# A list-scheduled beginning and one burst of k-v products per batch, in a linear-attention and SwiGLU kernel

## Chip, cores, metric

The kernel runs on one NeuronCore of a Trainium2 chip. The metric is the device time of one execution in microseconds (us), as the median of several. A trace's span is 1.8 us shorter than the device time of the same execution; positions below are us from the start of the span. Experiments ran on different chips, so each kernel is compared with the runs of the kernel before from its own rounds.

## The reference

Eight batches, eight heads, 576 positions, head size 64, float32 inputs. Cosine-weighted linear attention, then a SwiGLU block over 4608 tokens with d_model 512 and d_ff 1536:

```python
def phi(x, c, s):                       # c, s: cos and sin of pi/2 * position / S
    r = np.maximum(x, 0.0)
    return np.concatenate([r * c, r * s], axis=-1)
q_p = phi(q, cos_w, sin_w);  k_p = phi(k, cos_w, sin_w)
kv  = np.einsum('bhsf,bhsd->bhfd', k_p, v)
num = np.einsum('bhsf,bhfd->bhsd', q_p, kv)
den = np.einsum('bhsf,bhf->bhs', q_p, np.sum(k_p, axis=2))[..., None] + 1e-06
x   = (num / den)                       # then tokens x 512
g = x @ w_gate
out = (g / (1 + np.exp(-g)) * (x @ w_val)) @ w_out
```

## The kernel before

I read the program text as the schedule: in the traces an engine takes its instructions in the order in which the program issues them (in the changed kernel's first trace VectorE stands 2.37 us before a cast whose input is late, with a copy behind it in the text whose own input, matmul sums, is done by 11.0 us). PSUM stands in the program as eight banks of 512 float32 to a partition, and every matmul line of the traces writes to them (`banks<-`). 128 tokens make a tile, four tiles a token group; the first group (tiles 0 to 3, batch 0) is the beginning that the change rewrites. Banks of PSUM are handed out by hand:

```python
banks = psum.tile([P, 8, 512], FP32, name="banks")
def take(n, hold=None): ...       # the n banks used longest ago, in program order
```

The first loads, on SyncE's queue: v, then k and q in turns (q of slots 0 and 1 belongs to tile 0, slots 2 and 3 to tile 1; a slot is 64 positions). GpSimd's queue loads the weights with conversion to bf16, and q of slots 4 to 8 (tiles 2 and 3, and the last slot of the batch) between them. An FFN column is 128 of the 1536 columns of d_ff:

```python
load_first("v", slice(0, 2)); load_first("v", slice(2, 4))
load_first("k", slice(0, 2))
load_first("q", slice(0, G), 0, 2)
load_first("k", slice(2, 4))
load_first("q", slice(0, G), 2, 4)
# ... (cut)
load_w(0, 1); load_w(1, 1)                 # columns 0 and 1 of w_gate and w_val
load_slots(0, "q", CUT[0], NC)
for i in (2, 4, 6): load_w(i)
```

The beginning handles a tile at a time, with products of zeros (`idle_products`) where TensorE (PE) would wait:

```python
# ... (cut: ReLU of the first k, casts of the first q)
kv_first(0); turn_q(0); idle_products(4)
relu_first_k(2, "dve"); relu_first_k(3, "act", 5, NC); relu_first_k(3, "dve", 0, 5)
weight_q(0); kv_first(1); cast_q(2, "act")
a_tile(0, split=True); cast_q(3, "act"); idle_products(4)
x_turn(0, fast="split"); turn_q(1); weight_q(1)
for f in range(2): ffn_mm(0, f, 0, 2)      # FFN columns 0 and 1 of tile 0
a_tile(1)
# ... (cut: tiles 2 and 3 in the same way, each followed by FFN columns)
```

In the later batches the k-v products (36 matmuls of 64 x 64 for each half j of the heads) stand in two slots, one FFN column apart:

```python
def kv_mm(b, j):
    if j == 0: st[b, "kvps"] = take(2, ("kv", b))
    for c in range(NC):
        for i in range(2):
            for e in range(2):
                # ... (cut)
                nc.tensor.matmul(out=..., lhsT=raws[b, "k"][es, g, c], rhs=v2s[b % 2][es, g, c, :, 0:D1], ...)
# ... (cut)
tk = (s0 + 4, s0 + 5)
for j in range(J): at(tk[j], lambda b=b, j=j: kv_mm(b, j))
```

Of the kernel before, what the change touches and what calls it, by code (L numbers as in the profile page):

```python
# [17 lines left out]
def kernel(  # L18
# [86 lines left out]
    CUT = (4, 5)  # L105
# [11 lines left out]

    load_first("v", slice(0, 2))
    load_first("v", slice(2, 4))
    load_first("k", slice(0, 2))  # L120
    load_first("q", slice(0, G), 0, 2)
    load_first("k", slice(2, 4))
# [143 lines left out]
    def kv_mm(b, j):  # L266
        if j == 0:
            st[b, "kvps"] = take(2, ("kv", b))
        ps = st[b, "kvps"]
        for c in range(NC):  # L270
            for i in range(2):
                for e in range(2):
                    es = slice(e * SH, (e + 1) * SH)
                    g = 2 * j + i
                    nc.tensor.matmul(  # L275
                        out=ps[i * D:(i + 1) * D, e, j * 2 * D1:(j + 1) * 2 * D1],
                        lhsT=raws[b, "k"][es, g, c],
                        rhs=v2s[b % 2][es, g, c, :, 0:D1],
                        start=(c == 0), stop=(c == NC - 1),
                    )  # L280
# [22 lines left out]
    def kv_first(j):  # L303

        ps = take(2)
        for e in range(2):
            nc.tensor.matmul(out=ps[:, e, 0:4 * D1], lhsT=zeros,
                             rhs=zeros[:, 0:D1].unsqueeze(1).to_broadcast([P, 4, D1]), start=True, stop=False)
        pv = ps[:, :, 0:4 * D1].rearrange("p e (w i x) -> p e w i x", w=2, i=2)
        for c in range(NC):  # L310
# [9 lines left out]
        for e, eng in enumerate((nc.scalar.copy, nc.vector.tensor_copy)):  # L320
            eng(out=kvd[0][:, e, j].rearrange("p w i x -> p (w i x)"), in_=ps[:, e, 0:4 * D1])
# [10 lines left out]
    def turn_q(t):  # L332
        ps = take(1).bitcast(BF16).rearrange("p (y e s) -> p y e s", e=2, s=SH)
        for j in range(J):
            for c in range(2):
# [5 lines left out]
                for i in range(2):  # L341
                    nc.tensor.transpose(out=ps[i * D:(i + 1) * D, y].rearrange("p e s -> p (e s)"),
                                        in_=raws[0, "q"][:, 2 * j + i, 2 * t + c], identity=ident)
        nc.scalar.activation(out=qr[t % 2].rearrange("p e j c s -> p e (j c) s"),
                             in_=ps[:, 0:2 * J].rearrange("p y e s -> p e y s"), func=AF.Relu)

    def weight_q(t):
        for w in range(2):
            nc.vector.tensor_tensor(
                out=qwT[t % 2][:, w].rearrange("p e j c s -> p (e j) (c s)"),  # L350
                in0=qr[t % 2].rearrange("p e j c s -> p (e j) (c s)"),
                in1=tabq[:, w, 2 * t:2 * t + 2].rearrange("p c s -> p (c s)").unsqueeze(1).to_broadcast([P, 2 * J, P]),
                op=ALU.mult)

    def a_tile(t, split=False):
        ps = take(2)
        for j in range(J):
            for e in range(2):
                for w in range(2):
                    nc.tensor.matmul(  # L360
                        out=ps[:, e, 2 * j * D1:2 * (j + 1) * D1],
                        lhsT=qwT[t % 2][:, w, e, j].rearrange("p c s -> p (c s)"),
                        rhs=kvd[0][:, e, j, w].rearrange("p i x -> p (i x)"),
                        start=(w == 0), stop=(w == 1),
                    )
        x_of(t, ps, split)
# [19 lines left out]
    def x_of(t, ps, split=False):  # L386
        num = ps[:, :, 0:2 * J * D1].rearrange("p e (y x) -> p e y x", x=D1)
        den = smp.tile([P, H, 1], FP32, name="den")
        dv = den.rearrange("p (e y) o -> p e y o", e=2)
        nc.vector.tensor_single_scalar(out=dv, in_=num[:, :, :, D:D1], scalar=1e-6, op=ALU.add)  # L390
        rec = smp.tile([P, H, 1], FP32, name="rec")
        nc.vector.reciprocal(out=rec, in_=den)
        rv = rec.rearrange("p (e y) o -> p e y o", e=2)
        x = xp.tile([P, d_model], BF16, name="x")
        xv = x.rearrange("p (y e d) -> p e y d", e=2, d=D)
        for ys in (slice(0, 2), slice(2, 4)) if split else (slice(0, 4),):
            nc.vector.tensor_tensor(  # L397
                out=xv[:, :, ys], in0=num[:, :, ys, 0:D],
                in1=rv[:, :, ys].to_broadcast([P, 2, ys.stop - ys.start, D]), op=ALU.mult)
        st["x", t] = x  # L400
# [45 lines left out]
    def x_turn(t, fast=False):  # L446
        x = st.pop(("x", t))
        tg, off = divmod(t, GH // 2)
        if tg not in xT:
            xT[tg] = xtp.tile([P, GH // 2, KC, P], BF16, name="xT")  # L450
        o = xT[tg][:, off]
        if fast == "split":
            for ks, eng in ((slice(0, 2), nc.scalar.copy), (slice(2, 4), nc.vector.tensor_copy)):
                ps = take(1).bitcast(BF16).rearrange("p (k x) -> p k x", x=P)
                for kc in range(ks.start, ks.stop):
                    nc.tensor.transpose(out=ps[:, kc], in_=x[:, kc * P:(kc + 1) * P], identity=ident)
                eng(out=o[:, ks], in_=ps[:, ks])
        elif fast:
            ps = take(1).bitcast(BF16).rearrange("p (k x) -> p k x", x=P)
            for kc in range(KC):  # L460
                nc.tensor.transpose(out=ps[:, kc], in_=x[:, kc * P:(kc + 1) * P], identity=ident)  # L461
            nc.scalar.copy(out=o, in_=ps[:, 0:KC])
        else:
            nc.sync.dma_start_transpose(out=o, in_=x)


    def ffn_mm(tg, fc, lo=0, hi=GH):
# [3 lines left out]
        fs = slice(fc * P, (fc + 1) * P)  # L471
        if 2 * n <= 512:
            both = take(1)
            ps = [both[:, 0:n], both[:, n:2 * n]]
        else:
            ps = [take(1)[:, 0:n] for _ in range(2)]
        for o, w in zip(ps, (wg_sb, wv_sb)):
            for kc in range(KC):
                nc.tensor.matmul(out=o, lhsT=w[:, kc, fs], rhs=xT[tg][:, ts, kc],  # L479
                                 start=(kc == 0), stop=(kc == KC - 1))  # L480
        st["f", tg, fc, lo] = ps

    def ffn_act(tg, fc, lo=0, hi=GH):
        n = (hi - lo) * SH
        ps = st.pop(("f", tg, fc, lo))
        sg = sgp.tile([P, T], BF16, name="sg")
        nc.scalar.activation(out=sg[:, 0:n], in_=ps[0], func=AF.Silu)  # L487
        r = lo * SH
        nc.vector.tensor_tensor(out=hts[tg % 2][:, fc, r:r + n], in0=sg[:, 0:n], in1=ps[1], op=ALU.mult)  # L489

    def ffn_fc(*a):
        ffn_mm(*a)
# [42 lines left out]
    for g in range(1, G):  # L535
        nc.scalar.copy(out=raw_of(0, "v")[:, g], in_=first["v"][:, g])  # L536
    for g in range(G):
        vmul(0, g)
    hold = consts.tile([P, 1], FP32)
    hold2 = consts.tile([1, 2], BF16)  # L540
    nc.gpsimd.tensor_copy(out=hold, in_=first["v"][:, 1, 0, 0:1])
    load_w(0, 1)
    load_w(1, 1)
    load_slots(0, "q", CUT[0], NC)
# [3 lines left out]
    load_w(8)  # L548
    load_w(10)
# [3 lines left out]
    load_wo(1)  # L553
    load_slots(1, "q", CUT[1], NC)
    load_wo(2)
# [25 lines left out]
    relu_first_k(0, "act")  # L581
    relu_first_k(1, "dve")
    cast_q(0, "dve")
    cast_q(1, "dve")
    kv_first(0)
    turn_q(0)
    idle_products(4)
    relu_first_k(2, "dve")
    relu_first_k(3, "act", 5, NC)
    relu_first_k(3, "dve", 0, 5)  # L590
    weight_q(0)
    kv_first(1)
    cast_q(2, "act")
    a_tile(0, split=True)
    cast_q(3, "act")
    idle_products(4)
    x_turn(0, fast="split")
    turn_q(1)
    weight_q(1)
    for f in range(2):  # L600
        ffn_mm(0, f, 0, 2)
    a_tile(1)
    for f in range(2):
        ffn_act(0, f, 0, 2)
    turn_q(2)
    weight_q(2)
    ffn_fc(0, 2, 0, 2)
    x_turn(1, fast=True)
    ffn_fc(0, 3, 0, 2)
    a_tile(2)  # L610
    turn_q(3)
    ffn_fc(0, 0, 2, 4)
    ffn_fc(0, 1, 2, 4)
    weight_q(3)
    ffn_fc(0, 2, 2, 4)
    x_turn(2, fast=True)
    ffn_fc(0, 3, 2, 4)
    a_tile(3)
# [3 lines left out]
    for f in range(0, FC, 2):  # L622
        order += [("a", g) for g in ((4, 5, 6), (7, 8), (9, 10), (11,), (), ())[f // 2]]
        order += [("b", g) for g in (f, f + 1)]
    at("a5", turn(3, True))
    for j in range(J):
        at("b1", lambda j=j: qturn_pe(0, j, NC - 1, NC, "act"))
# [4 lines left out]
    at("b9", lambda: kv_mm(1, 0))  # L632
    at("b10", lambda: kv_mm(1, 1), lambda: kv_out(1))
    at("b11", q_(1, 0, 0), q_(1, 1, 0))
# [4 lines left out]
    at((1, 0), turn(4, True), q_(1, 0, 1), a_(6, 0))  # L639
    at((1, 1), a_(6, 1), q_(1, 1, 1))  # L640
    at((1, 2), turn(5, True), a_(7, 0))
    at((1, 3), a_(7, 1))
    at((2, 0), turn(6, True))
    at((2, 2), turn(7, True))
# [17 lines left out]
    for b in range(2, B):  # L662
# [15 lines left out]
        for j in range(J):  # L678
            at(tk[j], lambda b=b, j=j: kv_mm(b, j))
        at(tk[-1], lambda b=b: kv_out2(b))  # L680
# [54 lines left out]
```

## Time and profile before

| | before |
|---|---|
| median | 331.71 us |
| span of the profiled execution | 329.4 us |
| PE busy | 322.2 us (98%) |
| first FFN product / second token group starts | 15.03 / 58.92 us |
| from there to the end | 270.49 us |

Up to "the second token group starts" (the first FFN product with 512 columns) lies everything that the new list orders. From there to the end the program is the same in both kernels but for the k-v bursts. So a trace splits into two numbers that can be read apart. On PE's timeline of the kernel before (start, length, engine, line, operation): the first FFN product and the first of the second group; the prediction shows the other lines on which its reading rests.

```profile
15.03 0.52 PE L479 MATMUL banks<-xT,wg_sb 128*128 128x128 bf16 x4
58.92 1.03 PE L479 MATMUL banks<-xT,wg_sb 128*128 128x512 bf16 x4
```

### The profile page before, as it was taken

The numbers are of one execution on the slowest core, as the hardware profiler recorded it, in microseconds if no ns is written. First come the engines' busy times: TensorE is split into PE (matmuls) and PEld (weight loads), VectorE is DVE, ScalarE is ACT, GpSimd is POOL, SyncE is SP. The second block draws the span as 40 slices with busy tenths as digits, with TensorE's granted clock in tenths as the row PEclk, the third lists the DMA queues.
The fourth block names the chain that finished last, engine by engine and source line by source line (L and its number), as shares of the span: only waits on it lengthen the run. The fifth ranks groups of instructions, "written<-read, shape, count | busy, mean of one in ns | idle before, by whom it ended". The sixth has DMA issues, their size and how long they took to land.

```text
span 329.4 us, 6225 instructions
## 1 busy us (share of the span) xinstructions
PE 322.2 (98%) x2484; PEld 165.1 (50%) x2484; DVE 182.5 (55%) x366; ACT 134.3 (41%) x252; POOL 33.3 (10%) x56
## 2 busy tenths in 40 slices
PE   8889999999999999999999999999999999999995
PEld 4578855454445444544444444544454444444443
DVE  7775758685655755475556655664664145413420
ACT  7545457753364334433433434343432033213311
POOL 6654200002000200020002000200000000000000
PEclk9999999999999999999999999999999999999999
DMA  7999998298858797969597959795932411341014
GB/s 276 217 200 200 205 207 165 64 131 125 174 110 112 111 161 156 126 92 190 135 134 114 173 118 136 106 192 103 140 47 49 98 32 30 36 99 31 0 32 96
DMA packets 70860, 40.51 MB, mean 123 GB/s; under 512 B 45616, under 2 KB 65328, under 8 KB 70832
## 3 DMA queue, kind: packets, MB, share of 16 engines
q1 hardware_dynamic: 49536, 22.55, 39.2%
q0 software_dynamic: 21136, 17.44, 34.9%
q8 instruction: 19, 0.31, 0.4%
q10 hardware_dynamic: 160, 0.13, 0.1%
q14 instruction: 9, 0.07, 0.1%
HBM read 37.75 MB, written 9.44 MB: 143 GB/s over the span
## 4 chain that ended last, share of the span: by engine, by line
PE 89%; DMA 8%; POOL 1%; ACT 0%; ACTq 0%; issue 0%
PE banks L479 54%; PE banks L506 28%; DMA wv_sb<-in_moe_w_val_dram 4%; DMA wg_sb<-in_moe_w_gate_dram 3%; PE banks L275 3%; PE banks L379 2%; DMA wo_sb<-in_v_dram 1%; PE banks L414 1%; PE banks L525 0%; POOL wg_sb L200 0%; PE banks L461 0%; POOL wv_sb L201 0%; PE banks L261 0%; ACT ob L528 0%; POOL raw_q L101 0%
## 5 line engine op out<-in xcount | busy, mean ns | idle before, releaser
L489 DVE TENSOR_TENSOR ht<-sg,banks 128x512 bf16<-128x512 bf16 (+2 forms) x124 | 76.3, 617 | 73.8 <-PE banks L479 63.6
L487 ACT ACTIVATE sg<-banks 128x512 bf16<-128x512 f32 (+2 forms) x124 | 67.2, 542 | 117.5 <-PE banks L479 112.6
L479 PE MATMUL banks<-xT,wv_sb 128*128 128x512 bf16 (+2 forms) x496 | 113.7, 352 | 1.0 <-DMA wv_sb<-in_moe_w_val_dram 1.0
L479 PE MATMUL banks<-xT,wg_sb 128*128 128x512 bf16 (+2 forms) x496 | 113.9, 352 | 0.3 <-DMA wg_sb<-in_moe_w_gate_dram 0.3
L506 PE MATMUL banks<-wo_sb,ht 128*128 128x512 bf16 x420 | 94.3, 379 | 0.0
L479 PEld LDWEIGHTS <-wv_sb 128*128 128x128 bf16 x496 | 47.4, 98 | 47.7 <-DMA wv_sb<-in_moe_w_val_dram 1.5
L479 PEld LDWEIGHTS <-wg_sb 128*128 128x128 bf16 x496 | 45.5, 98 | 41.5 <-DMA wg_sb<-in_moe_w_gate_dram 0.4
L506 PEld LDWEIGHTS <-ht 128*128 128x128 bf16 x420 | 40.0, 98 | 45.4 <-issue 0.4
L513 ACT COPY ob<-banks 128x512 f32<-128x512 f32 x18 | 10.5, 585 | 51.6 <-PE banks L506 49.6
L229 DVE TENSOR_TENSOR r_q<-raw_q,tab 128x1152 bf16<-128x1152 bf16 x24 | 17.9, 753 | 20.2 <-ACT raw_q L212 20.2
L513 DVE COPY ob<-banks 128x512 f32<-128x512 f32 x17 | 11.7, 691 | 28.6 <-PE banks L506 27.6
L233 DVE TENSOR_TENSOR v<-raw_v,tab 128x1152 bf16<-128x1152 bf16 x31 | 22.9, 751 | 0.3 <-ACT raw_v L536 0.3
L397 DVE TENSOR_TENSOR x<-banks,rec 128x512 bf16<-128x512 f32 (+1 forms) x32 | 21.5, 674 | 1.1
L657 POOL COPY hold<-phit 1x2 bf16<-1x2 bf16 x5 | 0.9, 175 | 159.7 <-DMA phit<-r_q 159.7
L212 ACT ACTIVATE raw_k<-raw_k 128x576 bf16<-128x576 bf16 x24 | 16.0, 675 | 0.0
L212 ACT ACTIVATE raw_q<-raw_q 128x576 bf16<-128x576 bf16 x24 | 15.7, 680 | 0.3 <-DMA raw_q<-in_q_dram 0.3
L379 PEld LDWEIGHTS <-phit 128*128 128x128 bf16 (+1 forms) x240 | 9.9, 100 | 6.0 <-issue 1.3
L379 PE MATMUL banks<-kv,phit 128*128 128x65 bf16 (+1 forms) x240 | 11.5, 195 | 0.0
L275 PEld LDWEIGHTS <-raw_k 64*64 64x64 bf16 x504 | 7.8, 106 | 5.6 <-issue 4.7
L146 PE MATMUL banks<-zeros 128*128 128x64 bf16 (+1 forms) x64 | 9.6, 316 | 1.0 <-DVE zeros L141 1.0
L275 PE MATMUL banks<-v,raw_k 64*64 64x130 bf16 x504 | 10.2, 220 | 0.0
L298 DVE CAST kv<-banks 64x260 bf16<-64x260 f32 x12 | 5.1, 428 | 4.3 <-ACT kv L298 4.2
(82 smaller groups left out, 136.2 us busy)
## 6 DMA issues: line engine op xcount, KB each, us to landing
out_dram<-ob SPq DMA_DIRECT2D x70, 128.0 KB, 2.4
raw_k<-in_k_dram POOLq DMA_DIRECT2D x7, 576.0 KB, 10.8
raw_q<-in_q_dram POOLq DMA_DIRECT2D x6, 576.0 KB, 6.1
raw_v<-in_v_dram POOLq DMA_DIRECT2D x6, 576.0 KB, 13.1
wo_sb<-in_moe_w_out_dram POOLq DMA_DIRECT2D x3, 512.0 KB, 13.1
wg_sb<-in_moe_w_gate_dram POOLq DMA_DIRECT2D x5, 256.0 KB, 10.7
wv_sb<-in_moe_w_val_dram POOLq DMA_DIRECT2D x5, 256.0 KB, 10.9
wo_sb<-in_v_dram SPq DMA_DIRECT2D x2, 576.0 KB, 4.0
```

Of the source, the lines that this page charges most:

```text
L146: nc.tensor.matmul(out=ps, lhsT=zeros, rhs=zeros[:, 0:cols].unsqueeze(1).to_broadcast([P, 4, cols]), start=True, stop=True)
L212: nc.scalar.activation(out=out, in_=in_, func=AF.Relu)
L229: nc.vector.tensor_tensor(out=st[b, "q"][:, g], in0=o.unsqueeze(2).to_broadcast([P, NC, 2, D]), in1=tab, op=ALU.mult)
L233: nc.vector.tensor_tensor(out=v2s[b % 2][:, g, :, :, 0:D], in0=(first if b == 0 and g == 0 else {"v": raw_of(b, "v")})["v"][:, g].unsqueez ...
L275: nc.tensor.matmul(out=ps[i * D:(i + 1) * D, e, j * 2 * D1:(j + 1) * 2 * D1], lhsT=raws[b, "k"][es, g, c], rhs=v2s[b % 2][es, g, c, :, 0:D ...
L379: nc.tensor.matmul(out=ps[ms, e, g * D1:(g + 1) * D1], lhsT=phit[b][:, e, g, c:c + n].rearrange("p c s -> p (c s)"), rhs=kv2s[b % 2][:, e, ...
L397: nc.vector.tensor_tensor(out=xv[:, :, ys], in0=num[:, :, ys, 0:D], in1=rv[:, :, ys].to_broadcast([P, 2, ys.stop - ys.start, D]), op=ALU.mult)
L479: nc.tensor.matmul(out=o, lhsT=w[:, kc, fs], rhs=xT[tg][:, ts, kc], start=(kc == 0), stop=(kc == KC - 1))
L487: nc.scalar.activation(out=sg[:, 0:n], in_=ps[0], func=AF.Silu)
L489: nc.vector.tensor_tensor(out=hts[tg % 2][:, fc, r:r + n], in0=sg[:, 0:n], in1=ps[1], op=ALU.mult)
L506: nc.tensor.matmul(out=o_ps[t], lhsT=hts[tg % 2][:, fc, r:r + P], rhs=wo_sb[:, fc], start=(fc == 0), stop=(fc == FC - 1))
L513: (nc.scalar.copy if t % 2 == 0 else nc.vector.tensor_copy)(out=ob, in_=ps)
```

## The change

Its intent: to use PE's time in the first 20 us better by ordering all engines together, and to pay once per batch instead of twice what a burst of k-v products (64*64 tiling) costs between its neighbours (128*128): 0.24 us by the starts around 102 us in the trace of the kernel before. In four parts: SyncE's loads (q first, k's second half in two pieces); GpSimd's loads (q of slots 4 to 7 ahead of the weights); the beginning as one list of words, each an operation, with the engine behind `@`; and the k-v products in one burst. Some smaller moves come with them: the last slot of batch 0's q and one piece of w_out change their places among GpSimd's loads, and batch 1's loads and turns of q are cut differently.

```diff
     load_first("v", slice(2, 4))
+    load_first("q", slice(0, G), 0, 2)
     load_first("k", slice(0, 2))
-    load_first("q", slice(0, G), 0, 2)
-    load_first("k", slice(2, 4))
+    load_first("k", slice(2, 4), 0, KCUT)
+    load_first("k", slice(2, 4), KCUT, NC)
     load_first("q", slice(0, G), 2, 4)
 ... (cut)
+    load_slots(0, "q", CUT[0], NW)
     load_w(0, 1)
     load_w(1, 1)
-    load_slots(0, "q", CUT[0], NC)
 ... (cut: the old beginning goes, this list comes)
+        cq0@act cq1@act tq0 qr0@dve rk1.0@act rk0.0@dve qw0.0 qw0.1 z6 kv0.0 rk2.0@act rk3.0@dve rk2.1@act
+        kv1.0 kvo01@dve rk3.1@act cq3@dve kv1.1 cq2@dve kvo00@dve tq1 kvo10@act a0.0 qr1@dve kvo11@act qw1.1
+        z2 a0.1 qw1.0 tq2 den0 rec0 a1.0 x0.0 qr2@act tq3 x0.1 xt0.0 a1.1 qw2.0 xc0.0@act xt0.1 qw2.1
+        xc0.1@act den1 z2 a2.0 rec1 qr3@act G1.0 x1.0 a2.1 G0.0 s1.0 V0.0 qw3.0 s0.0 xt1.0 qw3.1 V1.0
 ... (cut)
-    def kv_mm(b, j):
-        if j == 0:
-            st[b, "kvps"] = take(2, ("kv", b))
-        ps = st[b, "kvps"]
-        for c in range(NC):
+    def kv_mm(b):
+        ps = st[b, "kvps"] = take(2, ("kv", b))
+        for j, c in [(j, c) for j in range(J) for c in range(NC)]:
 ... (cut)
-        for j in range(J):
-            at(tk[j], lambda b=b, j=j: kv_mm(b, j))
-        at(tk[-1], lambda b=b: kv_out2(b))
+        at(tk[-1], lambda b=b: kv_mm(b), lambda b=b: kv_out2(b))
```

The words that matter: `cq` cast of a q slot, `tq` turn (transpose) of a tile's q, `qr` its ReLU, `qw` its two weightings, `rk` ReLU of k, `kv` k-v products, `kvo` copy of their sums out of PSUM, `a` attention products, `den`, `rec`, `x` the division, `xt`/`xc` turn of x and its copy, `G`/`V`/`s`/`m` an FFN column's gate products, value products, silu and multiply, `z` products of zeros.

## The prediction

> **What bounds the kernel now.** I read the page first: busy time, then the chain that ended last, then TensorE's own timeline of the first 60 us.
>
> ```profile
> PE 322.2 (98%) x2484; PEld 165.1 (50%) x2484; DVE 182.5 (55%) x366; ACT 134.3 (41%) x252; POOL 33.3 (10%) x56
> PE 89%; DMA 8%; POOL 1%; ACT 0%; ACTq 0%; issue 0%
> ```
>
> TensorE (PE) is the bound, and 89% of the chain is PE. So a reordering can gain in only two ways: less PE time without useful products, or fewer losses between products. The 8% DMA of the chain lie in one place, as the chain in order of time shows (start, length, what):
>
> ```profile
> 18.02 12.22 DMA wv_sb<-in_moe_w_val_dram
> 30.24 0.05 issue
> 30.29 10.22 PE banks L479 x92
> ...
> 102.20 0.65 PE banks L275 x33
> 102.85 1.83 PE banks L479 x8
> 104.68 0.65 PE banks L275 x35
> 105.33 0.37 PE banks L379 x8
> ```
>
> From 30.29 us to the end the chain is PE almost without a hole. What can be gained at the beginning is what PE wastes before 30.29. PE's timeline there (start, length, instructions, wait before them):
>
> ```profile
> 10.34 1.03 PE L146 MATMUL banks<-zeros 128*128 128x512 bf16 x4
> 13.16 1.02 PE L146 MATMUL banks<-zeros 128*128 128x512 bf16 x4
> 17.78 0.40 PE L479 MATMUL banks<-xT,wg_sb 128*128 128x128 bf16 x4 [0.26 <-DMA wg_sb<-in_moe_w_gate_dram]
> 19.14 0.40 PE L479 MATMUL banks<-xT,wv_sb 128*128 128x128 bf16 x4 [0.96 <-DMA wv_sb<-in_moe_w_val_dram]
> 23.79 0.60 PE L479 MATMUL banks<-xT,wg_sb 128*128 128x256 bf16 x4
> ```
>
> A "busy" PE is not a useful one: L146 is products of zeros. So I count by starts. Groups of four follow each other by 0.22 us at 128 columns, 0.44 at 256, 0.86 at 512. The useful work between 8.36 us (the first real product) and 23.79 us: zero fills of the k-v banks 0.44; k-v products 2 x 0.65; turns of q 2 x 0.22 and 2 x 0.34; attention products of four tiles 4 x 0.45; turns of x 3 x 0.22; sixteen FFN groups of 128 columns 3.57. Sum 8.89 of 15.43 us. So 6.5 us are lost there (1.7 in eight products of zeros), and 0.25 more at the wait that ends at 30.29. From 23.79 to the second token group (L479 with 512 columns, from 58.92) there is 35.13 - 0.25 = 34.88 us of work. In all 43.77 us of useful PE work stand between 8.36 and that point.
>
> [...] the k-v products run in 64*64, their neighbours in 128*128. In the raw starts around 102 us, the last FFN product before a burst is followed after 0.309 us instead of 0.216, the first one behind it starts 0.151 us after the last k-v product, where k-v products follow each other by 0.014, and the next is 0.01 late. That is 0.09 + 0.14 + 0.01 = 0.24 us for each burst of 36. The chain shows its visible part: 1.83 for eight products that otherwise take 1.73.
>
> [...] the first loads through GpSimd, issued at 4.45, move their first packet at 8.77, and SyncE's last load is slow from there on; its 576 KB of the last k land at 11.0, 1.6 us after the load ahead of them, and the 256 KB of q behind them take 1.7 us more, less than half the rate:
>
> ```profile
> first_q<-in_q_dram SPq DMA_DIRECT2D x1, 256.0 KB, 9.3
> ```
>
> It was issued at 3.43, so it landed at 12.7. [...]
>
> **The change part by part.** (1) SyncE's loads: q of the first slots goes ahead of k, and k's second half is cut in two. The bytes ahead of the last k and the last q are the same, so I take their old landings, 11.0 and 12.7. The first half of k comes where q came, 9.4 instead of 8.5. q turns and weights then run in time that was a wait for k. (2) GpSimd's loads: q of slots 4 to 7 (256 KB as written) goes ahead of the weights, where slots 4 to 8 (320 KB) went behind the first four. The first four weight loads come about 1 us later (12.4 to 14.8 becomes about 13.4 to 15.8), the later ones not; no use of them is then earlier than its landing. (3) The beginning is written as one list for all engines; FFN starts later, with all of q's products squeezed ahead of it. Four tiles' FFN products after that point are the same columns, partly as 256 instead of 128, at the same cost per column. (4) The k-v products of each batch become one burst of 72; the turns of q of batch 1 go from four bursts to three, one beside the k-v burst.
>
> The beginning, step by step. VectorE (DVE) decides, since its order is fixed: it has the casts of the last q (slots 2 and 3) ahead of a copy of the k-v sums (kvd) without which tile 0 can't start. From q's landing, about 12.75, DVE does: two casts 0.75 (0.70 before), kvd copy 0.43, ReLU of the turned q 0.65 (an estimate: 0.60 on ScalarE, 0.68 for DVE reading 512 columns from the banks), two weightings 0.76, denominator, reciprocal and x of tile 0 1.19 (13.36 to 14.55 before), two weightings 0.76, the same three for tile 1 1.13 (17.21 to 18.34 before), two weightings 0.76, copy of the turned x of tile 1 about 0.5. Sum 6.9, so 19.7. The line that gives most of these:
>
> ```profile
> 12.54 0.43 DVE L321 CAST kvd<-banks 128x260 bf16<-128x260 f32 x1 [0.17 <-PE banks L314]
> 15.78 0.76 DVE L349 TENSOR_TENSOR qwT<-qr,tabq 128x512 bf16<-128x512 bf16 x2 [0.56 <-ACT qr L344]
> 17.65 0.69 DVE L397 TENSOR_TENSOR x<-banks,rec 128x512 bf16<-128x512 f32 x1
> ```
>
> From about 19.8 PE has two tiles and all weights that it needs next, and I see no further wait. By then it has done: fills 0.44, k-v 1.30, turns 1.12, four tiles' attention 1.80, two turns of x 0.44, four FFN groups 0.89: 5.99. What is left is 43.77 - 5.99 = 37.78, so the second token group starts at 57.6 instead of 58.9: 1.3 us gained, of 6.75 that were lost.
>
> The bursts: seven batches (1 to 7), one burst less each, 7 x 0.24 = 1.65 us; q's turns one or two switches less, about 0.2. All on PE, on the chain. Sum: 1.3 + 1.65 + 0.2 = 3.15 us, and 331.71 - 3.15 = 328.6. Everything behind 58.9 us is otherwise unchanged: the same products in the same order, and the same loads behind the same holds.
>
> **The rivals.** First, q's last load lands later than 12.7, because GpSimd's first packets are now of 512 B (40 ns each for 256 B before, 58 for 512)[...]. Each us of delay passes straight through DVE into the end; with 0.7 us the front gains 0.6 and the time is 329.3. For it: the packet times; against it: only 32 of them per engine.
> Second, q's last load lands earlier, near 11.5, which the list's author seems to have assumed (he puts its casts ahead of the copy). Most of its 16 parts did land between 10.2 and 11.5 and one at 12.4. Then the front gains about 2.5 and the time is 327.4. Against it: the same bytes in the same queue.
> Third, the gain of the front is given back: with the FFN earlier by 1 to 2 us, PE could wait for the weights of columns 10 and 11 (landing about 33) or for w_out (first part about 40 before, now 0.7 later). I find PE there at about 36 and 42.5, so it is hidden; otherwise only the bursts remain, 330.
> Fourth, the burst of 72 leaves ScalarE and DVE without FFN work for 1.2 us and the next bank comes late. DVE is 55% busy and the banks are held for a shorter time than before; I give it 0.2 us at most.
> Fifth, PE is so idle between 12 and 14 us that the clock is lowered. [...] the longest wait I see is 1.5, and before's clock stayed at 1.00 through a wait of 1 us.
>
> **Range and chances.** The bursts are measured: 1.3 to 1.9. The front is between -0.3 and +2.7. Together 327.2 to 330.3. Over 2% faster would be below 325.1, that is all 6.75 us of loss recovered at the front: 0.02. Slower by 2% needs a loss of 6.6 us, for which I see no cause: 0.01.
>
> **What would show it.** In the changed profile: k-v products in bursts of 72, one switch per batch, the chain without a piece of eight FFN products between two k-v pieces; DVE's cast of q with a wait on the q load until 12.7 and then no idle to 19; the first FFN product at about 17 instead of 15.0, yet no wait for wv_sb after that; the second token group at 57.6; and from there to the end 270.5 less about 1.45 us (six of the seven bursts). It is wrong if PE waits on weights or on a bank after 20 us, or if the distance from the second group to the end does not shrink.

Sum: 1.3 us for the beginning, 1.65 for seven bursts (0.24 each, from the raw starts), 0.2 estimated for the turns of q, 3.15 in all, so 328.6. What makes a burst cost 0.24 us inside PE was not shown. For the slow last loads the trace of the kernel before shows this: from 8.2 to 8.9 us SyncE's queue moved 0.27 MB nearly alone (144 packets, 4 of GpSimd's queue), and from 9.7 to 10.5, with 227 packets of GpSimd's beside 208 of its own, 0.12 MB. How the DMA engines share their time between the two was not shown. That an idle PE lowers the clock, the fifth rival, was the author's estimate: no trace had shown it yet.

## The result, and the profile after

The changed kernel takes 327.65 us (327.52 to 327.92, four runs), the kernel before in the same rounds 331.62 us (331.18 to 332.31). The ratio is 0.988, 95% interval 0.9861 to 0.9898. A ratio here is formed by the comparison from the fast runs of both kernels in the same rounds, so it is not quite the ratio of the medians. The interval leaves out 1, so a gain is there. 328.6 was predicted with a range of 327.2 to 330.3: inside it, on the fast side.

Busy time and the chain that ended last, by engine, of the kernel after:

```profile
PE 318.7 (98%) x2459; PEld 165.0 (51%) x2470; DVE 182.3 (56%) x367; ACT 132.8 (41%) x248; POOL 34.1 (10%) x57
PE 94%; DMA 3%; SPq 1%; issue 0%; ACT 0%; DVE 0%; ACTq 0%; DVEq 0%
```

PE is still the bound. Busy PE fell by 3.5 us, and the DMA share of the chain from 8% to 3%. The chain in order of time (start, length, what) shows which load is left, and the burst of batch 3:

```profile
3.84 9.83 DMA first_q<-in_q_dram
13.76 0.60 DVE qf L339 x2
...
101.90 1.17 PE banks L276 x65
103.43 3.45 PE banks L503 x16
```

The weights of the old chain (until 30.24) are gone. In their place stands one load, the q of tile 1 (slots 2 and 3), until 13.7, with VectorE (DVE) behind it. The k-v pieces are one of 1.17, without FFN products between. On PE's timeline (start, length, products, and in brackets the wait and what ended it):

```profile
11.96 0.73 PE L316 MATMUL banks<-v,raw_k 64*64 64x130 bf16 x16 [0.31 <-ACT raw_k L215]
14.40 0.40 PE L347 MATMUL banks<-ident,qf 128*128 128x128 bf16 x4 [1.71 <-DVE qf L339]
...
18.07 0.39 PE L503 MATMUL banks<-xT,wg_sb 128*128 128x128 bf16 x4
...
57.13 1.03 PE L503 MATMUL banks<-xT,wg_sb 128*128 128x512 bf16 x4
```

The first FFN product comes 3 us later than before (18.07), yet the second group starts 1.79 us earlier (57.13 instead of 58.92), because PE has no hole between 17.8 and there. From there to the end the span has 269.02 us instead of 270.49, that is 1.47 less. 1.79 + 1.47 = 3.26 us, the difference of the two spans. The medians differ by 3.97: the profiled execution of the kernel before (331.19) was one of its fastest, that of the kernel after (327.92) its slowest.

DVE behind that load (start, length, instruction):

```profile
13.76 0.58 DVE L339 CAST qf<-first_q 128x256 bf16<-128x256 f32 x2 [2.37 <-DMA first_q<-in_q_dram]
14.27 0.41 DVE L324 CAST kvd<-banks 128x260 bf16<-128x260 f32 x1
14.84 0.42 DVE L217 TENSOR_SCALAR qr<-banks 128x512 bf16<-128x512 bf16 x1 [0.15 <-PE banks L347]
...
19.45 0.42 DVE L324 COPY xT<-banks 128x512 bf16<-128x512 bf16 x1
```

DVE waits 2.37 us for q and then works without a pause over 0.15 us until the turned x of tile 1 is copied at 19.87: 6.1 us after the load.

### The profile page after: what moved, and what is told of

It is laid out like the page before. It is cut to its first block, busy times and chain, and to the rows that moved or that the text cites. A ratio compares the mean times of both kernels' runs of the same rounds, so it can differ in the third digit from the quotient of the medians.

```text
span 326.1 us, 6192 instructions
## 1 busy us (share of the span) xinstructions
PE 318.7 (98%) x2459; PEld 165.0 (51%) x2470; DVE 182.3 (56%) x367; ACT 132.8 (41%) x248; POOL 34.1 (10%) x57
## 4 chain that ended last, share of the span: by engine, by line
PE 94%; DMA 3%; SPq 1%; issue 0%; ACT 0%; DVE 0%; ACTq 0%; DVEq 0%
PE banks L503 57%; PE banks L539 28%; DMA first_q<-in_q_dram 3%; PE banks L276 3%; PE banks L390 2%; SPq L116 1%; PE banks L475 1%; PE banks L434 1%; PE banks L372 1%; PE banks L558 1%; PE banks L264 0%; PE banks L149 0%; ACT ob L561 0%; PE banks L351 0%; DVE qf L339 0%
## 5 line engine op out<-in xcount | busy, mean ns | idle before, releaser
L390 PE MATMUL banks<-kv,phit 128*128 128x65 bf16 (+1 forms) x240 | 11.5, 195 | 0.0
L276 PE MATMUL banks<-v,raw_k 64*64 64x130 bf16 x504 | 8.7, 218 | 0.0
```

What stands on the lines that cost most here:

```text
L276: nc.tensor.matmul(out=ps[i * D:(i + 1) * D, e, j * 2 * D1:(j + 1) * 2 * D1], lhsT=raws[b, "k"][es, g, c], rhs=v2s[b % 2][es, g, c, :, 0:D ...
L390: nc.tensor.matmul(out=ps[ms, e, g * D1:(g + 1) * D1], lhsT=phit[b][:, e, g, c:c + n].rearrange("p c s -> p (c s)"), rhs=kv2s[b % 2][:, e, ...
```

## The experiments

Twelve experiments ran: ten further kernels, and the changed kernel twice more. The table has, for each trace, when the casts of tile 1's q began, when the second token group started, and what was left from there to the end of the span, then the times of all runs, and how many of them had a mean granted clock under 0.996 (the granted clock is the share of its full speed that TensorE's clock has, by the profile). In burst_alone and the three tile1_last lists the casts of that q are on ScalarE, as in the kernel before (12.81).

| kernel | casts of q | second group | rest | median us | before, same rounds | ratio to before (95%) | runs with low clock |
|---|---|---|---|---|---|---|---|
| changed kernel, first | 13.76 | 57.13 | 269.02 | 327.65 | 331.62 | 0.988 (0.9861 to 0.9898) | 0 of 4 |
| burst_alone | 12.41 | 58.76 | 269.10 | 329.96 | 331.13 | 0.9973 (0.9957 to 0.9989) | 1 of 6 |
| two_bursts | 12.98 | 57.66 | 270.38 | 329.40 | 331.13 | 0.9945 (0.9927 to 0.9963) | 2 of 6 |
| four_bursts | 13.54 | 56.82 | 272.45 | 331.04 | 331.13 | 0.9994 (0.9982 to 1.0006) | 0 of 5 |
| weights_first | 13.23 | 59.54 | 269.00 | 330.39 | 331.13 | 0.9971 (0.994 to 1.0003) | 4 of 6 |
| after_again | 12.56 | 56.10 | 269.00 | 328.15 | 331.56 | 0.9896 (0.9874 to 0.9918) | 3 of 6 |
| keep_warm | 13.14 | 56.70 | 269.02 | 327.93 | 331.56 | 0.9891 (0.9874 to 0.9909) | 0 of 5 |
| copy_first | 13.32 | 56.60 | 269.00 | 327.86 | 331.56 | 0.9888 (0.9871 to 0.9905) | 0 of 5 |
| tile1_last | 15.89 | 56.92 | 269.00 | 327.69 | 331.56 | 0.9883 (0.9867 to 0.99) | 0 of 4 |
| q_ahead | 12.51 | 60.34 | 268.99 | 330.78 | 331.35 | 0.9969 (0.9942 to 0.9997) | 5 of 6 |
| tile1_last2 | 15.16 | 57.97 | 269.03 | 329.16 | 331.35 | 0.9929 (0.9904 to 0.9954) | 0 of 6 |
| tile1_last3 | 15.10 | 55.63 | 269.00 | 326.69 | 331.26 | 0.9855 (0.9831 to 0.9879) | 0 of 4 |
| after_third | 14.01 | 58.40 | 269.03 | 328.31 | 331.26 | 0.9891 (0.9863 to 0.9918) | 3 of 6 |

All gave correct results. All these runs count as fast runs in the sense of the comparison; the low clock is told apart below.

### burst_alone: the kernel before with one burst per batch, and nothing else

```diff
-    at("b9", lambda: kv_mm(1, 0))
-    at("b10", lambda: kv_mm(1, 1), lambda: kv_out(1))
+    at("b10", lambda: kv_mm(1), lambda: kv_out(1))
 ... (and kv_mm and its slot for batches 2 to 7 as in the change)
```

> The kernel before with one thing of the change: the k-v products of a batch as one burst of 72 (seven batches). Theory 1 [...]: 7 x 0.24 = 1.65 us less than before, so about 330.0 against 331.6, and all of it in the span after the start. Theory 2 (the switch is hidden or an artefact of modelled matmul ends, and the whole gain of the change lies in the beginning): 331.6, no difference.

Theory 1 is the 0.24 us per burst that the prediction read from the starts.

It takes 329.96 against 331.13, 1.2 us less by the medians. In the trace the rest after the second group is 269.10 instead of 270.49: 1.39 us for six bursts, and the second group starts 0.16 us earlier. Theory 2 falls: the bursts alone bring a third of the gain by the medians, nearly half by the traces. It is less than the 1.65 us that were expected: by the ratio's interval 0.4 to 1.4 us. So the times alone show that there is a gain, and the 1.39 us of the trace show its size.

### two_bursts and four_bursts: the changed kernel with its burst cut up again

```diff
-        at(tk[-1], lambda b=b: kv_mm(b), lambda b=b: kv_out2(b))
+        for part in range(4 if b > 2 else 1):
+            at(s0 + 5 - (3 - part if b > 2 else 0), lambda b=b, part=part: kv_mm(b, part, 4 if b > 2 else 1))
+        at(tk[-1], lambda b=b: kv_out2(b))
```

(That is four_bursts; two_bursts puts two parts into the two slots of before, for batches 2 to 7.)

> The changed kernel with the k-v products of batches 2 to 7 in two bursts again, one slot apart, the new beginning kept. Theory 1: 6 x 0.24 = 1.45 us more than the changed kernel, about 329.1, and the second token group still starts at 57.1 in the trace. Theory 2: 327.7.

> The changed kernel with the k-v products of batches 3 to 7 in four bursts of 18 in four slots (batches 1 and 2 in one burst): the suspected cost, multiplied. Theory 1: 5 batches x 3 more bursts x 0.24 = 3.6 us more than the changed kernel, 331.25. Theory 2: 327.7. If a burst of 72 gained only through what it did to the order of the other engines, the cost would not grow in proportion to the number of bursts.

The rest grows from 269.02 to 270.38 with six more bursts (0.227 us each) and to 272.45 with fifteen more (0.229 each). With the 1.47 us that the change took off for six (0.245 each), three steps of different size give nearly one cost per burst. PE's timeline of four_bursts around one cut:

```profile
164.81 0.34 PE L279 MATMUL banks<-v,raw_k 64*64 64x130 bf16 x12
165.08 1.04 PE L506 MATMUL banks<-xT,wg_sb 128*128 128x512 bf16 x4
165.96 1.03 PE L506 MATMUL banks<-xT,wv_sb 128*128 128x512 bf16 x4
166.91 0.48 PE L279 MATMUL banks<-v,raw_k 64*64 64x130 bf16 x20
```

A burst of these is 16 or 20 products (the 72 are cut after 16, 36 and 52); some records are missing (12 of 16 in the first). The starts tell it: eight FFN products of 0.216 us should take 1.73, but 166.91 - 165.08 is 1.83, and the k-v products' own 20 x 0.014 = 0.28 us take 167.33 - 166.91 = 0.42 with the way out: 0.10 + 0.14 = 0.24. The whole time, 331.04, is back at that of the kernel before, as 331.25 was expected. In two_bursts the second group started at 57.66, not at 57.1 or earlier: that is another matter, and it became the main finding.

### A lowered clock in the beginning

In the trace of two_bursts the granted clock, which is 1.00 in the same place of the first trace of the changed kernel, falls to a half. Busy time by stretch (stretch, PE, weight loads, DVE, ACT, POOL, granted clock, DMA share, GB/s), of two_bursts:

```profile
12.00:14.00 2.00, 0.18 (x4) 0.18 (x4) 1.02 (x3) 0.52 (x2) 1.03 (x2) 1.00 1.78 181
14.00:16.00 2.00, 2.00 (x24) 1.33 (x22) 1.74 (x7) 0.00 (x1) 1.19 (x2) 0.72 1.62 192
16.00:18.00 2.00, 2.00 (x21) 1.62 (x21) 1.51 (x5) 0.97 (x2) 1.54 (x3) 0.50 1.45 196
```

First PE stands almost still for 2 us, waiting for the last q; then it works 3.4 us at half speed (clock 0.50, from 14.9 to 18.3). So the same kernel was run twice more, to count this, and once with zeros in the wait.

> The changed kernel itself once more, for how often its beginning is hit by a lowered clock. In the traces of two variants of it the granted clock fell to 0.50 between 14 and 20 us, after a stretch from 12.3 to 14 us in which TensorE waits for the last q. Theory A (that wait of about 2 us, longer than any of the kernel before, lowers the clock in some executions): some of the runs have a clock under 0.997 and are 1 to 2.5 us slower than the others (327.6), so that the median is 328 to 329. Theory B (those variants were hit by chance): all runs within 0.5 us of 327.7, clock 0.998 to 1.0.

> The changed kernel again, on the same chip and in the same rounds as tile1_last3, to compare the two, and to count once more the runs with a lowered clock. Expected: 327.0 to 327.7 where the clock is at least 0.998, 328.4 to 329.4 where it is 0.993 to 0.995, some of each; second token group 43.3 to 43.6 us after the casts of the last q.

Six of the twelve runs had a clock of 0.993, and they took 328.57 to 329.21 us; the six others 326.69 to 328.05. The two groups do not overlap. In the first measurement none of four was hit. The full-clock runs spread wider than expected, and after_third's own trace, being hit, has 44.39 us from the casts to the second group. The trace of after_third is one of those hit:

```profile
12.18:15.59 3.41, 1.70 (x27) 1.09 (x28) 1.39 (x5) 0.90 (x3) 1.74 (x3) 1.00 1.73 186
15.59:19.00 3.41, 3.41 (x34) 2.42 (x33) 2.82 (x10) 1.14 (x3) 2.71 (x4) 0.50 1.46 194
```

The clock is at a half for exactly 3.41 us. In the 3.41 us before, PE was busy 1.70 us.

Why half of the runs, and not all? The wait alone does not tell: after_again waited longest (2.00 us) and kept its clock, after_third waited 1.66 us and lost it. The records of the granted clock in the traces show one thing more. Full clock lasts from 5.94 to 326.79 us in the first trace of the changed kernel and from 6.55 to 330.81 in that of the kernel before: 320.85 and 324.27 us, 94 and 95 times 3.413. In all 14 traces each stretch at full clock between two changes is such a whole number long (10.24, 307.20, 310.61, 317.44, 320.85, 324.27 us), while the first rise lies anywhere between 3.7 and 7.0 us. If one counts in steps of 3.413 us from that rise, the wait falls into one step in some runs and across two in others. These are the steps that hold it, or most of it, in the layout of the fence above, of two_bursts, four_bursts (two steps), after_again and weights_first:

```profile
11.46:14.88 3.42, 1.44 (x26) 0.98 (x27) 1.71 (x5) 0.65 (x2) 1.90 (x3) 1.00 1.72 187
10.15:13.56 3.41, 2.26 (x76) 1.34 (x74) 1.15 (x4) 1.67 (x5) 1.19 (x2) 1.00 1.53 199
13.56:16.98 3.42, 2.86 (x41) 2.06 (x42) 3.16 (x11) 0.68 (x2) 2.50 (x5) 1.00 1.61 191
11.68:15.10 3.42, 1.72 (x23) 1.18 (x23) 2.35 (x7) 0.41 (x2) 2.23 (x3) 1.00 1.74 184
10.53:13.95 3.42, 2.07 (x77) 1.28 (x66) 1.70 (x6) 1.55 (x5) 1.00 (x3) 1.00 1.65 192
```

The clock fell at the end of the first and the last of them and held through the others. So where the steps lie, which differs from run to run, may decide, but PE's busy time in a step does not decide alone: the clock fell after 2.07 us in weights_first and held after 1.72 in after_again and 1.76 in the first trace of the changed kernel (12.76 to 16.17). In the step of weights_first most products are the small k-v ones of 64 x 64; whether these count for less was not tested.

The kernel before has such runs too: 0.992 to 0.994 in 12 of its 44 runs beside these experiments, 331.35 to 333.04 us where the others take 330.65 to 331.90, so the ranges overlap only a little. No trace of one was taken, so where its clock falls stays open.

### keep_warm: zeros in the wait

```diff
-        kv1.0 kvo01@dve rk3.1@act cq3@dve kv1.1 cq2@dve kvo00@dve tq1
+        kv1.0 kvo01@dve rk3.1@act cq3@dve kv1.1 z6 cq2@dve kvo00@dve tq1
```

> The changed kernel with six products of zeros (1.3 us) in TensorE's wait for the last q, after the last k-v products of batch 0. Theory A: no run with a lowered clock, all runs at 327.3 to 327.9, and the second token group at 56.5 to 57.1. Theory B: no difference from the changed kernel of the same rounds. If q lands earlier than 13.7 the zeros end before it (about 13.7), so they cost nothing or at most 0.3 us.

No run of five has a low clock; they take 327.43 to 328.29 us (up to 327.9 was expected), the changed kernel in the same rounds 326.88 to 329.16. The slow half is gone, the spread is 0.9 instead of 2.3 us, and the median falls by only 0.2: its untroubled runs are not faster than those of the changed kernel (327.86 in the mean against 327.37). With five and three runs whose ranges overlap, that difference stays open; that only runs with a short wait escape is not the reason, since after_again's trace escaped with the longest. Together with copy_first and the three tile1_last lists, all with zeros in their waits, no run of 24 had a clock under 0.997, against 8 of 27 with the changed kernel's beginning as it is (6 of 16 of its own, 2 of 6 of two_bursts, none of 5 of four_bursts); q_ahead below has zeros in the wrong place and is hit in five of six.

### copy_first, q_ahead, weights_first: what sets the beginning

copy_first moves the copy of the k-v sums on DVE ahead of the casts that wait for q, on top of keep_warm:

```diff
-        rk3.1@act cq3@dve kv1.1 z6 cq2@dve kvo00@dve tq1
+        rk3.1@act kvo00@dve cq3@dve kv1.1 z6 cq2@dve tq1
```

> As keep_warm, with the copy of the first half of the k-v sums on VectorE ahead of the casts of the last q instead of behind them. If VectorE's fixed order behind the last q sets the beginning, as the prediction had it, the 0.41 us of the copy leave that path: the second token group starts 0.4 us earlier for the same landing of q, time about 0.4 us below keep_warm. Rival: TensorE and the x of tile 0 wait for something else (the second half of the k-v sums, from ScalarE), then no difference.

Inconclusive. The second group starts 43.28 us after the casts of q instead of 43.55 in keep_warm, but four_bursts, with the old order, has 43.28 too, and the times don't resolve it (327.86 against 327.93). The table gives a stronger sign for what sets the beginning. In the five traces with the changed kernel's list, or nearly so, and no low clock, the second group follows the casts by 43.28 to 43.55 us, while the casts begin anywhere from 12.56 to 13.76. When q lands is passed on to the second group almost to the full.

weights_first puts GpSimd's q load behind the first four weight loads again:

```diff
-    load_slots(0, "q", CUT[0], NW)
     load_w(0, 1)
     load_w(1, 1)
+    load_slots(0, "q", CUT[0], NW)
```

> The changed kernel with GpSimd's load of q slots 4 to 7 behind the first four weight loads again. It asks why q's last SyncE load landed at 13.7 and not at the 12.7 of before. Theory 1 [...]: it lands at 12.7 to 12.9 again. Theory 2 (SyncE's own smaller packets of k and its later issue): it stays at 13.6 to 13.8. The time: the turn of tile 2 must now wait for its q until about 16.1 instead of starting at 15.7, so I expect 327.6 to 328.2, no gain.

Theory 1 blames GpSimd's first packets, which the traces show as 59 ns each in the changed kernel (512 B, 87 packets from 8.9 to 9.7 us) and 40 ns in the kernel before (256 B, 129 packets).

The line of the last q load (size, us from issue to landing), the changed kernel's first and weights_first's second:

```profile
first_q<-in_q_dram SPq DMA_DIRECT2D x1, 256.0 KB, 9.8
```

```profile
first_q<-in_q_dram SPq DMA_DIRECT2D x1, 256.0 KB, 9.3
```

It lands 0.5 us sooner after its issue. But two_bursts, with the changed kernel's loads, has 9.1, and after_again 8.6. The same load varies by more than the effect asked for, so these single traces can't tell which of the two theories holds. The time is clearer: tile 2 waits for its q, the first FFN product is at 20.44, and four of six runs are hit by the low clock. The mean of the other two is 328.42. The order of the change is the better one.

q_ahead loads the last q ahead of the last piece of k, on top of keep_warm:

```diff
+    load_first("q", slice(0, G), 2, 4)
     load_first("k", slice(2, 4), KCUT, NC)
-    load_first("q", slice(0, G), 2, 4)
```

> As keep_warm, with SyncE's load of the last q (slots 2 and 3) ahead of the second piece of the last k. In the runs so far the second token group starts 43.3 to 43.6 us after VectorE begins the casts of that q, wherever they begin between 12.6 and 13.8. Theory (the landing of the last q sets the beginning): q lands about 0.8 to 1 us earlier and the k piece takes its place, so the path goes over to the k piece (ReLU 0.8, k-v products 0.3, two copies on ScalarE 0.65); second group 0.4 to 0.9 us earlier than keep_warm, about 55.9 to 56.3, time about 327.3. Rival: the k piece is then as late as q was and costs more behind it: second group at 56.7 or later.

It loses. q came at 12.51, but now PE waits for k, and the zeros stand behind that wait:

```profile
14.23 0.73 PE L316 MATMUL banks<-v,raw_k 64*64 64x130 bf16 x16 [2.25 <-ACT raw_k L215]
```

The clock falls at 15.2, the second group is at 60.34. The one untroubled run takes 329.08. Of the last two loads only the one put ahead came early here, and PE waited 2.25 us for the other; what can change is who needs them.

### tile1_last, tile1_last2, tile1_last3: nobody but tile 1 waits for the last q

Only tile 1 needs the last q, but in the changed list DVE holds back tile 0 behind its casts (from 13.76 us, the copy of tile 0's k-v sums only at 14.27). These lists take tile 0 through first, then tiles 2 and 3, then tile 1. Of tile1_last3:

```diff
-        kv1.0 kvo01@dve rk3.1@act cq3@dve kv1.1 cq2@dve kvo00@dve tq1 kvo10@act a0.0 qr1@dve kvo11@act qw1.1
-        z2 a0.1 qw1.0 tq2 den0 rec0 a1.0 x0.0 qr2@act tq3 x0.1 xt0.0 a1.1 qw2.0 xc0.0@act xt0.1 qw2.1
+        kv1.0 kvo01@dve rk2.1@act kvo00@dve rk3.1@dve a0.0 kv1.1 kvo10@act kvo11@dve z3 a0.1 den0 rec0 tq2 x0.0
+        qr2@act x0.1 tq3 qr3@act xt0.0 qw2.0 qw2.1 xc0.0@act xt0.1 xc0.1@act cq2@act cq3@act a2.0 a2.1
 ... (cut)
```

> A new list for the beginning that does not let tile 0 wait for the last q at all: tile 0 goes through as soon as its k-v sums are copied, then tiles 2 and 3 (their q comes with GpSimd's first load, landed at 13.0), then tile 1, whose q lands last. Theory (the path through the landing of the last q and VectorE behind it sets the beginning): first FFN product at about 15.5 instead of 18.1, second token group at about 55.3 to 56.0, time 326.0 to 326.8. Rival: the weights become the wait (columns 2 and 3 land at 17.6 and 18.9): then TensorE waits for them and the second group is not before 56.7.

A miss: second group at 56.92, no better than the changed kernel. My list had zeros in the way and an FFN group ahead of tile 2's attention.

> The list of tile1_last mended where its trace showed self-made waits: two products of zeros stood before the second k-v part of batch 0 (0.4 us) and four in front of tile 2 (0.9 us), VectorE waited 0.6 us for tile 2's products because they stood behind an FFN group, and the copy of tile 2's x stood on ScalarE behind a silu. Theory: those 1.9 us come off and the second token group is at 55.0 to 55.6, time 325.9 to 326.5, with a clock of 1.00. Rival: the weights of columns 1 to 3 (16.4 to 18.9) set the beginning and it stays at 56.5 or more.

A worse miss, 329.16: the FFN started at 15.64, but I had put each silu between the gate and the value products of a pair, which share a bank, so that the value products wait for ScalarE (four waits over 0.15 us, 1.72 us in all; the fifth that the next text counts is for the copy of an x). PE's timeline:

```profile
19.03 0.38 PE L503 MATMUL banks<-xT,wv_sb 128*128 128x128 bf16 x4 [0.36 <-ACT sg L509]
...
20.49 0.38 PE L503 MATMUL banks<-xT,wv_sb 128*128 128x128 bf16 x4 [0.63 <-ACT sg L509]
```

> tile1_last2 with its one self-made fault mended: there the silu of a pair stood between its gate and its value products, which share a bank, and TensorE waited 0.36 to 0.63 us for ScalarE five times (2.1 us). Here the silu stands behind both, tile 1's attention comes earlier, and the x of tile 3 is turned in the wait for the copy of tile 2's. Theory (the landing of the last q and VectorE behind it set the changed kernel's beginning, and tile 1 alone needs that q): no wait of TensorE above 0.2 us after 18.5, second token group at 55.4 to 56.0, time 326.2 to 326.9, clock 0.998 to 1.0 in all runs. Rival: weights of columns 1 to 3, or VectorE itself, set it, and it stays at 56.5 or more.

With the silu behind both, the list does what it was made for. PE's timeline of tile1_last3, first FFN product and the only wait after it up to 20 us:

```profile
15.59 0.38 PE L503 MATMUL banks<-xT,wg_sb 128*128 128x128 bf16 x4
...
18.01 0.40 PE L475 MATMUL banks<-ident,x 128*128 128x128 bf16 x4 [0.23 <-DVE x L411]
```

The second group starts at 55.63, and the time is 326.69 us (326.35 to 327.09), no run with a low clock, against 328.31 of the changed kernel and 331.26 of the kernel before in the same rounds. It beats the kernel before clearly. Against the changed kernel the sign is weaker: its ratio to before, 0.9855, lies under the changed kernel's 0.9891, but the intervals overlap; its slowest run (327.09) lies under five of the changed kernel's six. Of runs at full clock alone the means are 326.70 and 327.32 (four and three runs, their ranges overlap), so some 0.6 us of the 1.6 come from the shorter path and the others from the clock that no longer falls. The weights, the rival, did not bind: no wait of PE for them over 0.15 us is in the trace.

## Why the prediction was right, point by point

**The bursts were right, within 0.02 us each.** 0.24 us per burst from the raw starts; the rest shrank by 0.245 for each of six in the changed kernel and by 0.232 in burst_alone, and grew by 0.23 for each of 6 and 15 added. The prediction asked for 1.45 us off the rest, 1.47 came. The 0.2 us for the turns of q of batch 1 were not measured alone.

**The beginning was right in mechanism and its two main terms were off in opposite directions.** The step "so I take their old landings, 11.0 and 12.7" failed: tile 1's q came at 12.6 to 14.0, in the first trace 13.7. This is the first rival of the prediction; its cause (GpSimd's larger packets, 59 ns instead of 40, or SyncE's own smaller ones) stays open. The step "Sum 6.9, so 19.7" was too long: DVE needed 6.1 us from the casts to the copy of tile 1's x (casts 0.58 instead of 0.75, ReLU of the turned q 0.42 instead of the estimated 0.65, copy 0.42 instead of 0.5, and some 0.3 because most of its instructions start about 0.08 us before the one ahead has ended, which a sum of durations counts twice). In the first trace the two errors cancel, which is luck: the copy ended at 19.87, and at that time PE had done what the prediction put there. It had been without a hole since 17.8. Expected for the second group was 57.6 less 0.24 for batch 1's burst and 0.2 for its turns, 57.16; the trace has 57.13. The first FFN product was expected at about 17 and came at 18.07, since q came 1 us late. The stated range, 327.2 to 330.3, is narrower at its slow end than its own terms: -0.3 and 1.3 us make 330.7.

**Why the time was lower than predicted.** The first trace was of the slowest of four runs. Where q came at 12.56, the second group started at 56.10. In the experiments' rounds the runs of the changed kernel at full clock took 327.37 and 327.32 in the mean and those of the kernel before 331.39 and 331.21: 3.9 to 4.0 us, of which 1.7 are bursts (seven times 0.24) and the others the beginning. So the beginning gave about 2.3 and not 1.5 (1.3 and the turns): the term that was mis-sized is the path behind q, 43.3 to 43.6 us from cast to second group where the prediction had 44.4 (57.16 - 12.75).

**The rivals.** The second (q near 11.5) did not come, the earliest was 12.56. The third did not either: no wait for weights after 20 us. The fourth costs nothing that shows in the rest. The fifth was dismissed wrongly. "The longest wait I see is 1.5" was 1.7 to 2.0 in the three traces of the changed kernel, and in half of the runs on two chips the clock fell, at about 1.5 us each (328.82 and 328.89 in the mean against 327.37 and 327.32). The four runs of the first measurement escaped it, which is luck too: the same kernel, hit half of the time, has medians of 328.15 and 328.31 on other chips, which also lie in the range.

## What to carry to other kernels

Where PE is the bound, look for switches between tilings and bring products of one tiling together: here each burst of 64*64 products among 128*128 ones cost 0.23 to 0.245 us, in and out together, and it could be read from the starts of neighbouring products before any experiment. In a list-scheduled beginning, ask of each in-order engine which late load stands in front of work that does not need it; putting only the dependent tile behind it took another 1.6 us off the median, some 0.6 of it by the shorter path. Look for waits of PE like those of 1.7 to 2.0 us here: with products of zeros in them no run of 24 had a lowered clock, against 8 of 27 without (though keep_warm took only 0.2 us off the median). And judge a beginning by several runs with their clocks: after_again's trace has the full clock, and three of the six runs beside it had not.
